# First two batches' last queries beside their last keys, w_ch1 behind the values, and the first four batches' pieces and loads in another order

## The chip, the cores and the metric

The kernel runs on one core of a Trainium2 chip. A core has TensorE for matmuls (PE in the profile; PEld is its weight load), VectorE (DVE), ScalarE (ACT), GpSimd (POOL) and SyncE (SP, which here only issues DMAs), 16 DMA engines, an on-chip memory SBUF of 128 partitions and an accumulator memory PSUM that matmuls write to. Each engine works through its own list of instructions in order and waits on semaphores. The metric is the device time of one execution in microseconds (us); lower is better.

## The reference

Linear attention with a cosine weighting, then a mixer over tokens and channels, for 8 batches of 576 tokens, 8 heads of 64.

```python
def phi(x, c, s):                       # c, s: cosine and sine of the token's place
    r = np.maximum(x, 0.0)
    return np.concatenate([r * c, r * s], axis=-1)
q_p = phi(q, cos_w, sin_w)
k_p = phi(k, cos_w, sin_w)
kv = np.einsum('bhsf,bhsd->bhfd', k_p, v)
z = np.sum(k_p, axis=2)
num = np.einsum('bhsf,bhfd->bhsd', q_p, kv)
den = np.einsum('bhsf,bhf->bhs', q_p, z)[..., None] + 1e-06
x = num / den                           # then 576 tokens x 512 channels for each batch
xt = x.transpose(0, 2, 1)
h = np.maximum(xt @ w_tok1, 0.0) @ w_tok2      # 576 -> 256 -> 576
u = x + h.transpose(0, 2, 1)
h2 = np.maximum(u @ w_ch1, 0.0) @ w_ch2        # 512 -> 1536 -> 512
out = u + h2
```

Inputs and outputs are float32; matmuls are bfloat16 with float32 sums.

## The kernel before, in words

**Tiles.** The 576 tokens of a batch are four chunks (0 to 3) of 128 and a tail (R) of 64. The tails of two batches share one tile of 128 partitions: rows 0 to 63 for the even batch, 64 to 127 for the odd one (`half(b % 2)`). `kp`, `qp` are the features of keys and queries (128 for a head), `v_aug` the values with a column of ones, so that `kv_ps` carries the sum of keys too. `qpT` are the turned queries, `x` the attention output, `B` the inner tokens of the mixer, `u` the residual, `uT` its transpose, `h1T` the inner channels (12 of them, `NCH`).

**Stages.** Batch b's channel mixer (`Channel`) is a list of steps: 12 of `c_step` (four matmuls of 512 columns into `c_ps`, then ScalarE's `h1T`; odd batches also carry the tail pair's `c_tail`), then `o_step` pieces of two matmuls. Batch b+1's attention and token mixer (`Front.pieces`) is cut into pieces, and a plan says at which slot (step) of batch b each is issued; C is slot 0 and O slot 12. So the order on every engine is written out by hand. KS and QS make the features of a chunk of keys or queries (cosine and sine half; with True the sine half goes to ScalarE), V casts values, KV adds a chunk to `kv_ps`, QT turns queries on TensorE, `q_trans_dma` by a DMA issued from SP, N makes `num_ps` and x, `mix_head` and `mix_tail` are the first token product, T the second with `u`, and `u_trans_dma` makes `uT`. Even and odd batches have plans of their own; batch 2, whose loads come late, has the plan "late" with V at slots 6, 6, 7, 7, 7 and KV at 7, 7, 8, 8, 8, where the odd plan has V at -1, -1, 0, 1, 2 and KV at 2 to 6.

**The first front.** Batch 0's attention has no stage to lie beside; `first_front` writes it out: q features and TensorE transposes in halves of four heads, the q tail, the keys chunk by chunk with `ksum`, then `dens` (q times the key sum, all 40 columns into `d_ps`), kv by halves of the heads (lo on ScalarE, hi on VectorE to `kv_sb`), five `num` with the x multiplication on VectorE, tok1, B, transposes to `uT` and the first three `c_ps` by blocks. `busy` issues matmuls of zeros that fill TensorE's pauses.

**Loads.** SP's queue issues most loads; w_ch1 and w_ch2, which are cast on the way, go through GpSimd's queue. `after` makes one load wait for another: w_ch1 for the second half of k 0, batch 1's k for the second part of w_ch1, batch 2's k for the second of three parts of w_ch2. `load_batch` is called at given steps. PSUM has four banks in `ps_mm` and two pairs in `ps_at`.

Of the kernel before, what the change touches and what calls it, by code (L numbers as in the profile page):

```python
# [16 lines left out]
def kernel(  # L17
# [76 lines left out]

    def tiles():
        return tuple(io.tile([P, H, R * D], F32, name=n) for n in ("qt", "vt", "kt"))
# [9 lines left out]
    load_tail(qtt0, q, 0)  # L106
    load_main(kt0, k, 0, 0, HH)
    k_done = load_main(kt0, k, 0, HH, H)
# [3 lines left out]
    load_main(vt0, v, 0, HH, H)  # L112
# [3 lines left out]
    w_tok1n = stage1[:, 0:R * D_tok].rearrange("p (r t) -> p r t", r=R)  # L116
    w_tok2n = stage2[:, 0:NT * S].rearrange("p (n s) -> p n s", n=NT)
# [37 lines left out]
    v_augs, x_tails = [], []  # L155
    for i in range(2):
        va = const.tile([P, NSC, H, DP], BF16, name=f"v_aug{i}")
        nc.vector.memset(va[:, 0:R, :, D:D1], 1.0)
        nc.vector.memset(va[half(1 - i), R, :, :], 0.0)
        nc.vector.memset(va[half(i), R, :, D:D1], 1.0)  # L160
        v_augs.append(va)
        xt = const.tile([P, Dm], BF16, name=f"x_tail{i}")
        nc.vector.memset(xt[half(1 - i), :], 0.0)
        x_tails.append(xt)
# [15 lines left out]
    for t in (tail0.kp, tail0.qp):  # L180
        nc.gpsimd.memset(t[half(1)], 0.0)
    for g in range(2):
        nc.gpsimd.dma_start(out=w_tail1[half(g), :], in_=moe_w_tok1[SM:S, :])
# [8 lines left out]
    after(w_ch1_done[0], k_done)  # L192
    w_ch2_done = []
    def load_w_ch2(third):
        ki = third * NCH // 3
        w_ch2_done.append(nc.gpsimd.dma_start(
            out=w_ch2[:, ki:ki + 4, :],
            in_=moe_w_ch2[ki * P:(ki + 4) * P, :].rearrange("(n t) d -> t n d", t=P)))
# [10 lines left out]
    def permute_tok2(ki):  # L209
        nc.scalar.copy(w_tok2[:, ki, 0:SM].rearrange("t (r p) -> t r p", r=R),  # L210
                       w_tok2n[:, ki, 0:SM].rearrange("t (p r) -> t r p", r=R))
        nc.scalar.copy(w_tok2[:, ki, SM:].rearrange("t (g s) -> t g s", g=2),
                       w_tok2n[:, ki, None, SM:S].to_broadcast([P, 2, ST]))


    class Front:
        def __init__(self, b, res, tail):
            self.qt, self.vt, self.kt = io_tiles[b]
            self.va, self.xt = v_augs[b % 2], x_tails[b % 2]
            self.res, self.tail = res, tail  # L220
            self.rows = half(b % 2)


            self.alone = b < 2
            self.kp, self.qp = {}, {}
# [20 lines left out]
        def feature(self, which, ci, j, heads=(0, H), on_act=False):  # L246
# [8 lines left out]
            else:  # L255
                t = self.tail
                dst, src = (t.kp, t.kt) if which == "k" else (t.qp, t.qt)
                rows = self.rows if self.alone else slice(0, P)
                w, o_ap, i_ap = w[rows], dst[rows, lo:hi, j, :], src[rows, lo:hi, :]
            if on_act:  # L260
                nc.scalar.activation(o_ap, i_ap, AF.Relu, bias=bias0[0:w.shape[0]], scale=w)
# [33 lines left out]
        def dens(self, ci):  # L295

            if ci == 0:
                self.d_ps = ps_mm.tile([P, NSC * H], F32, name="d_ps", tag="mm")
                self.d_sb = small.tile([P, NSC * H, 1], F32, name="d_sb")
            for h in range(H):  # L300
                i = ci * H + h
                nc.tensor.matmul(self.d_ps[:, i:i + 1], self.qT_of(ci, h),
                                 self.ks_sb[:, h:h + 1], start=True, stop=True)

        def dens_out(self, lo, hi):
            nc.vector.tensor_scalar_add(self.d_sb[:, lo:hi, 0], self.d_ps[:, lo:hi], 1e-6)
            nc.vector.reciprocal(self.d_sb[:, lo:hi, 0], self.d_sb[:, lo:hi, 0])

        def kv(self, ci, halves=(0, 1)):
            if ci == 0 and not hasattr(self, "kv_ps"):  # L310
                self.kv_ps = {}
                if halves == (0, 1):
                    both = ps_at.tile([P, 2, 512], F32, name="kv_ps", tag="at")
                    self.kv_ps = {g: both[:, g, :] for g in range(2)}
            if ci == 0 and halves != (0, 1):
                for g in halves:
                    self.kv_ps[g] = ps_at.tile([P, 2, 512], F32, name="kv_ps", tag="at")[:, 0, :]
# [10 lines left out]
        def kv_out(self, halves=(0, 1)):  # L328
            for g in halves:
                copy = nc.vector.tensor_copy if g else nc.scalar.copy  # L330
# [16 lines left out]

        def q_trans_dma(self, ci):
# [4 lines left out]
        def num(self, ci, fill=0, dens=False):  # L353
            num_ps = ps_at.tile([P, 2, 512], F32, name="num_ps", tag="at")
            if fill:
                busy(num_ps[:, 0, HH * DP:512], 1)
            for h in range(H):
                g, j = divmod(h, HH)
                nc.tensor.matmul(num_ps[:, g, j * DP:j * DP + D1], self.qT_of(ci, h),  # L359
                                 self.kv_sb[g][:, j, 0:D1], start=True, stop=True)  # L360
            rows = self.rows_of(ci)
            nv = num_ps[rows, :, 0:HH * DP].rearrange("p g (j d) -> p g j d", d=DP)
            if dens:
                den = self.d_sb[rows, ci * H:(ci + 1) * H, :].rearrange("p (g j) o -> p g j o", g=2)
            else:
# [3 lines left out]
            nc.vector.tensor_mul(  # L369
                self.x_of(ci)[rows].rearrange("p (g j d) -> p g j d", g=2, j=HH),  # L370
                nv[:, :, :, 0:D], den.to_broadcast([rows.stop - rows.start, 2, HH, D]))
# [89 lines left out]
        def pieces(self, b, before):  # L461
# [3 lines left out]
            first, odd, late = b == 1, b % 2 == 1, b == 2  # L465
# [3 lines left out]
            if first:  # L469

                u, act, pool = before.tok2, nc.scalar, nc.gpsimd
                plan = [(4, KS, 0), (4, KS, 1), (5, u, 0, ps_at, False), (5, KS, 2, True),
                        (6, KS, 3, True), (6, u, 1, ps_at, False), (7, KS, R), (7, V, R, nc.vector), (8, V, 0, act),
                        (8, V, 2, pool), (8, load_w_ch2, 0), (8, V, 3, pool),
                        (8, load_w_ch2, 1), (8, load_w_ch2, 2),
                        (8, u, 2, None, False), (9, V, 1, act), (9, u, 3, None, False),
                        (9, QS, 0), (10, u, R, None, False)]
                plan += [(11, KV, ci) for ci in range(NSC)]
                plan += [(11, QS, 1), (11, QS, 2), (11, self.kv_out),
                         (11, QT, 0, (0, H), act, ps_at), (11, QT, 1), (11, QS, R),  # L480
                         (O, QT, 2), (O, N, 0), (O, QS, 3), (O + 1, QT, R),
                         (O + 1, N, 1), (O + 3, N, 2), (O + 3, QT, 3),
                         (O + 5, N, R), (O + 7, N, 3), (O + 8, before.tail_cast)]
            else:
# [21 lines left out]
            if first:  # L506
                at, mix, t = (), O + 7, O + 11
            elif odd:
                at, mix, t = (C + 8, C + 9, C + 10, C + 11, O + 2), O + 3, O + 7
            elif late:  # L510
                at, mix, t = (C + 10, C + 11, O + 1, O + 2, O + 4), O + 5, O + 9
# [20 lines left out]
    class Channel:  # L532
# [59 lines left out]
        def steps(self, done):  # L592
# [43 lines left out]
    def first_front(f):  # L636
# [24 lines left out]
        busy(idle_ps, 2)  # L661
        f.ksum(R)
        busy(idle_ps, 1)
        for ci in range(R):
            if ci == 2:
                f.ksum_out()
            f.values(ci, nc.scalar, lo_heads)
        cast_tok1(0)
        f.values(R, nc.vector)
        for ci in range(R):  # L670
            f.values(ci, nc.vector, hi_heads)
        for ci in (0, 1, 2):
            f.dens(ci)
# [3 lines left out]
        for ci in (R, 3):  # L677
            f.dens(ci)
        f.dens_out(0, NSC * H)
# [9 lines left out]
        f.num(ORDER[0], fill=1, dens=True)  # L689
        f.num(ORDER[1], dens=True)  # L690
# [23 lines left out]
    def load_batch(b, which="kvq", behind=None, main=True, tails=True):  # L714
# [7 lines left out]
        for n in which:  # L722
# [7 lines left out]
            if tails and (b % 2 == 0 or b == 1):  # L730
                load_tail(tail_dst, src, b | 1)
        return done
# [3 lines left out]
    load_batch(1, "kvq", behind=w_ch1_done[1])  # L736
# [9 lines left out]
    c = first_front(fronts[0])  # L746
    slots = next_front(1)
    for b in range(B):
# [4 lines left out]
        for i, step in enumerate(steps):  # L753
# [54 lines left out]
```

## Time and profile before

| | us |
|---|---|
| median of 3 runs (269.6 to 270.21) | 270.06 |
| profiled execution, its own time | 270.61 |
| its span, first to last instruction | 268.8 |
| TensorE busy | 260.0 (97%) |
| VectorE busy | 164.9 (61%) |
| ScalarE busy | 129.9 (48%) |
| GpSimd busy | 10.9 (4%) |
| TensorE on the chain that ended last | 86% |
| DMA, mean over the span | 200 GB/s |
| granted TensorE clock | 1.00 |

A page of the profile comes from one execution. Busy time is the union of an engine's instructions; a matmul's end is modelled, so back-to-back matmuls overlap by some 0.2 us in the records, and the pace is read from start to start. The chain is followed back from the last instruction to what released it. In the timeline each row has start, duration, engine, line of the kernel, instruction, out<-in, shape and count; what stands in brackets is the engine's idle time before it and what ended it. A DMA's time to landing counts from its issue.

### The profile page before, as it was taken

The page shows a single profiled execution, that of the slowest core. Times are in us where ns is not written, and L with a number is a line of the kernel's source. Part 1 is how long each engine was busy: PE and PEld are TensorE (multiplying, and loading weights), DVE is VectorE, ACT ScalarE, POOL GpSimd, SP SyncE. Part 2 cuts the span into 40 slices and gives each one's busy share as a digit, 9 for nine tenths or more (in the row PEclk, how much of TensorE's full clock was granted, in tenths as well). Part 3 has the DMA queues.
Part 4 walks back from the last instruction along what each step waited for, and adds up shares of the span by engine and source line. Part 5 has one row for each costly group of instructions (what it writes and reads, how often), then busy time and mean ns, then how long its engine had stood idle before and what let it go on. Part 6 is the DMA issues. An engine that isn't in the chain of part 4 may idle for free.

```text
span 268.8 us, 5101 instructions
## 1 busy us (share of the span) xinstructions
PE 260.0 (97%) x2029; PEld 139.2 (52%) x2050; DVE 164.9 (61%) x376; ACT 129.9 (48%) x228; POOL 10.9 (4%) x24
## 2 busy tenths in 40 slices
PE   7989999999999999999999999999999999999994
PEld 2565465455544455446644455446644455445543
DVE  6874798794366747777466747776565846720022
ACT  4954975528606272446606372546606362526400
POOL 6300220000000000000000000000000000000000
PEclk9999999999999999999999999999999999999999
DMA  6999999589999999469984989189974580180032
GB/s 217 342 277 275 333 162 285 211 210 253 179 316 289 251 208 319 146 166 266 182 307 117 287 207 355 54 179 254 229 261 117 156 120 0 53 202 3 2 107 88
DMA packets 91815, 53.68 MB, mean 200 GB/s; under 512 B 59408, under 2 KB 86928, under 8 KB 91792
## 3 DMA queue, kind: packets, MB, share of 16 engines
q1 hardware_dynamic: 88432, 49.62, 69.5%
q0 software_dynamic: 2832, 3.21, 7.2%
q10 hardware_dynamic: 528, 0.52, 0.6%
q8 instruction: 16, 0.26, 0.4%
q14 instruction: 7, 0.06, 0.1%
HBM read 35.85 MB, written 9.44 MB: 168 GB/s over the span
## 4 chain that ended last, share of the span: by engine, by line
PE 86%; DVE 6%; DMA 3%; ACT 3%; issue 1%; DVEq 0%; ACTq 0%
PE o_ps L579 33%; PE c_ps L546 25%; PE u_ps L406 7%; PE b_ps L382 6%; PE ct_ps L566 3%; PE kv_ps L320 3%; PE num_ps L359 3%; DVE x_sb L369 3%; DMA qt<-in_q_dram 2%; DVE qp L263 1%; ACT h1T L550 1%; PE qT_ps L340 1%; DMA qpT_tail<-qp_tail 1%; PE idle_ps L204 1%; ACT v_aug L274 1%; PE c_ps L556 1%
## 5 line engine op out<-in xcount | busy, mean ns | idle before, releaser
L579 PE MATMUL o_ps<-w_ch,h1T 128*128 128x512 bf16 (+1 forms) x380 | 92.6, 372 | 0.6
L546 PE MATMUL c_ps<-uT,w_ch 128*128 128x512 bf16 (+2 forms) x384 | 92.2, 372 | 0.1
L550 ACT ACTIVATE h1T<-c_ps 128x512 bf16<-128x512 f32 x93 | 55.5, 599 | 60.5 <-PE c_ps L546 60.1
L579 PEld LDWEIGHTS <-h1T 128*128 128x128 bf16 x396 | 37.3, 98 | 39.5 <-issue 0.2
L546 PEld LDWEIGHTS <-w_ch 128*128 128x128 bf16 x384 | 33.5, 97 | 29.5 <-issue 0.2
L584 DVE TENSOR_TENSOR o_sb<-o_ps,u_sb 128x512 f32<-128x512 f32 (+1 forms) x33 | 22.3, 674 | 29.5 <-PE o_ps L579 29.4
L409 DVE TENSOR_TENSOR u_sb<-u_ps,x_sb 128x512 f32<-128x512 f32 x32 | 21.7, 689 | 6.0 <-PE u_ps L406 5.6
L413 ACT CAST u_bf<-u_sb 128x512 bf16<-128x512 f32 x28 | 17.3, 620 | 16.7 <-DVE u_sb L409 16.7
L406 PE MATMUL u_ps<-B,w_tok 128*128 128x512 bf16 x79 | 22.4, 379 | 0.2
L387 ACT ACTIVATE B<-b_ps 128x512 bf16<-128x512 f32 x8 | 4.8, 598 | 33.7 <-PE b_ps L382 33.5
L369 DVE TENSOR_TENSOR x_sb<-num_ps,den 128x512 bf16<-128x512 f32 x28 | 19.4, 691 | 1.0
L566 PEld LDWEIGHTS <-w_ch 128*128 128x128 bf16 x192 | 14.0, 98 | 9.2
L382 PE MATMUL b_ps<-x_sb,w_tok 128*128 128x512 bf16 x63 | 17.7, 379 | 0.1
L263 DVE TENSOR_SCALAR kp<-kt,cos_t 128x512 bf16<-128x512 f32 x32 | 15.2, 481 | 3.8 <-DMA kt<-in_k_dram 3.8
L566 PE MATMUL ct_ps<-uT_tail,w_ch 128*128 128x128 bf16 x192 | 17.2, 219 | 0.0
L274 ACT CAST v_aug<-vt 128x512 bf16<-128x512 f32 (+1 forms) x30 | 16.8, 587 | 0.1
L263 DVE TENSOR_SCALAR qp<-qt,cos_t 128x512 bf16<-128x512 f32 (+1 forms) x35 | 15.9, 455 | 0.5 <-DMA qt<-in_q_dram 0.5
L263 DVE TENSOR_SCALAR qp<-qt,sin_t 128x512 bf16<-128x512 f32 (+1 forms) x35 | 15.9, 455 | 0.0
L359 PEld LDWEIGHTS <-qpT 128*128 128x128 bf16 x256 | 11.5, 98 | 6.1 <-issue 1.1
L584 DVE TENSOR_TENSOR o_sb<-o_ps,u_tail 128x512 f32<-128x512 f32 x4 | 2.8, 692 | 19.0 <-PE o_ps L579 19.0
L359 PE MATMUL num_ps<-kv_sb,qpT 128*128 128x65 bf16 x256 | 13.0, 193 | 1.3 <-DVE x_sb L369 0.5
L331 DVE CAST kv_sb<-kv_ps 128x260 bf16<-128x260 f32 x8 | 3.5, 433 | 16.6 <-ACT kv_sb L331 16.5
(93 smaller groups left out, 228.6 us busy)
## 6 DMA issues: line engine op xcount, KB each, us to landing
out_dram<-o_sb SPq DMA_DIRECT2D x31, 256.0 KB, 2.9
kt<-in_k_dram SPq DMA_DIRECT2D x7, 1024.0 KB, 6.6
vt<-in_v_dram SPq DMA_DIRECT2D x7, 1024.0 KB, 6.6
qt<-in_q_dram SPq DMA_DIRECT2D x7, 1024.0 KB, 8.4
w_ch<-in_moe_w_ch_dram POOLq DMA_DIRECT2D x4, 384.0 KB, 10.2
w_ch<-in_moe_w_ch_dram POOLq DMA_DIRECT2D x3, 512.0 KB, 7.5
out_dram<-o_sb SPq DMA_DIRECT2D x10, 128.0 KB, 2.3
qtt<-in_q_dram SPq DMA_DIRECT2D x8, 128.0 KB, 5.3
```

The source lines that it names most:

```text
L263: nc.vector.tensor_scalar(o_ap, i_ap, scalar1=w, scalar2=0.0, op0=ALU.mult, op1=ALU.max)
L274: nc.scalar.copy(dst, src)
L359: nc.tensor.matmul(num_ps[:, g, j * DP:j * DP + D1], self.qT_of(ci, h), self.kv_sb[g][:, j, 0:D1], start=True, stop=True)
L369: nc.vector.tensor_mul(self.x_of(ci)[rows].rearrange("p (g j d) -> p g j d", g=2, j=HH), nv[:, :, :, 0:D], den.to_broadcast([rows.stop - r ...
L382: nc.tensor.matmul(self.b1_ps[mi], w, self.x_of(ci), start=(ci == ORDER[0]), stop=(ci == ORDER[-1]))
L406: nc.tensor.matmul(u_ps, w_tok2[:, ki, ci * P:(ci + 1) * P], self.B1[:, ki, :], start=(ki == 0), stop=(ki == NT - 1))
L409: nc.vector.tensor_add(u, u_ps[rows], self.x_of(ci)[rows])
L546: nc.tensor.matmul(c_ps[:, lo:hi], w_ch1[:, ki, mi * P:(mi + 1) * P], uT[:, lo // P:hi // P, ki, :], start=(ki == 0), stop=(ki == NCC - 1))
L550: nc.scalar.activation(self.h1T[:, mi, :], c_ps, AF.Relu)
L566: nc.tensor.matmul(self.ct_ps[:, mi % R, :], w_ch1[:, ki, mi * P:(mi + 1) * P], self.tail.uT[:, ki, :], start=(mi % R == 0 and ki == 0), s ...
L579: nc.tensor.matmul(o_ps, h, w_ch2[:, ki, cols], start=ki == 0, stop=ki == NCH - 1)
L584: nc.vector.tensor_add(o_sb, o_ps, u)
```

## The change

Batch 0's and 1's query tails no longer have a tile and a pass of their own: `load_beside` puts them into the free half of the key tail's tile, the key features of the tail run on all 128 rows, and `q_trans_beside` turns the other half's rows with transposes of 64 columns. In the first front the keys follow the queries at once, chunk 0 in halves; the sines of chunks 1 to 3 are ScalarE's; the value casts, `kv_sb` copies and weight casts are shared among VectorE, ScalarE and GpSimd in another way; `dens` runs in one piece before kv, and the first two chunks' `num` and x are made by halves of the heads. w_tok1's tail is loaded by SP in float32 and cast by GpSimd; w_ch1 waits for the values instead of the keys. In batch 0's stage the five tok2 pieces come first, keys and values a slot or more later, q 0's sine goes to ScalarE, w_ch2 comes in four parts, and the first two o chunks alternate by one step instead of two. Batch 3 gets the late plan; the late plan's QS R moves from slot 6 to 9. The loads of batches 2, 3 and 4 change places: batch 2's q tail behind the first turned queries, batch 3's v from step 9 to step 24 of batch 1, batch 4's k from there to step 4 of batch 2.

The diff, cut to its core:

```diff
+    def load_beside(dst, src, b):
+        return nc.sync.dma_start(out=dst[half(1 - b)],
+                                 in_=src[b, :, SM:S, :].rearrange("h s d -> s h d"))
...
-    load_tail(qtt0, q, 0)
+    load_beside(ktt0, q, 0)
...
+    for g in range(2):
+        nc.sync.dma_start(out=w_tail1n[half(g), :], in_=moe_w_tok1[SM:S, :])
...
-    after(w_ch1_done[0], k_done)
+    after(w_ch1_done[0], v_done)
...
+        def q_trans_beside(self):
+
+            g = self.rows.start // ST
+            rows = half(1 - g)
+            qT_ps = ps_mm.tile([P, H, ST], BF16, name="qT_ps", tag="mm")
+            for h in range(H):
+                nc.tensor.transpose(qT_ps[:, h, :],
+                                    self.tail.kp[rows, h, :, :].rearrange("p a b -> p (a b)"),
+                                    ident[rows, rows])
+            nc.scalar.copy(self.tail.qpT[:, :, half(g)], qT_ps)
...
-            first, odd, late = b == 1, b % 2 == 1, b == 2
+            first, odd, late = b == 1, b % 2 == 1, b in (2, 3)
...
-                plan = [(4, KS, 0), (4, KS, 1), (5, u, 0, ps_at, False), (5, KS, 2, True),
-                        (6, KS, 3, True), (6, u, 1, ps_at, False), (7, KS, R), (7, V, R, nc.vector), (8, V, 0, act),
-                        (8, V, 2, pool), (8, load_w_ch2, 0), (8, V, 3, pool),
-                        (8, load_w_ch2, 1), (8, load_w_ch2, 2),
-                        (8, u, 2, None, False), (9, V, 1, act), (9, u, 3, None, False),
-                        (9, QS, 0), (10, u, R, None, False)]
+                plan = [(4, u, 0, ps_at, False), (5, u, 1, ps_at, False), (5, KS, 0),
+                        (6, u, 2, None, False), (6, KS, 1), (7, u, 3, None, False),
+                        (7, KS, 2, True), (8, u, R, None, False), (8, KS, 3, True),
+                        (9, V, R, nc.vector), (9, KS, R), (9, V, 0, act),
+                        (10, V, 2, pool), (10, load_w_ch2, 0, 2), (10, V, 3, pool),
+                        (10, load_w_ch2, 2, 4), (10, load_w_ch2, 4, 8),
+                        (10, load_w_ch2, 8, NCH), (10, V, 1, act), (11, QS, 0, True)]
...
-                             (2, QS, 1), (3, QS, 2), (4, QS, 3), (5, KS, R), (6, QS, R))
+                             (2, QS, 1), (3, QS, 2), (4, QS, 3), (5, KS, R), (9, QS, R))
...
-                for lo in range(0, NCH, 4):
+                for lo in range(0, NCH, 2):
                     for ci in (0, 1):
-                        o_range(ci, lo, lo + 4)
+                        o_range(ci, lo, lo + 2)
...
-        f.q_side(R)
-        f.q_trans(R, pool=ps_at)
-        busy(idle_ps, 2)
-        for ci in range(R):
+        for heads in (lo_heads, hi_heads):
+            f.feature("k", 0, 0, heads)
+            f.feature("k", 0, 1, heads)
+        busy(idle_ps, 4)
+        f.ksum(0)
+        for ci in range(1, R):
             f.feature("k", ci, 0)
-            f.feature("k", ci, 1, on_act=(ci > 1))
-            busy(idle_ps, 2)
+            f.feature("k", ci, 1, on_act=True)
+            busy(idle_ps, 2 if ci < 3 else 1)
             f.ksum(ci)
         f.k_side(R)
...
+        f.ksum_out()
+        f.q_trans_beside()
         for ci in range(R):
...
+            f.values(ci, nc.vector if ci < 2 else nc.scalar, lo_heads)
         f.values(R, nc.vector)
         for ci in range(R):
-            f.values(ci, nc.vector, hi_heads)
...
+            f.values(ci, nc.vector if ci < 3 else nc.scalar, hi_heads)
+        den = f.dens(range(NSC))
+        f.dens_out(*den)
         for ci in range(NSC):
             f.kv(ci, (0,))
         f.kv_out((0,))
...
-        f.kv_out((1,))
-        cast_tok1(1)
-        for ki in range(NT):
-            permute_tok2(ki)
+        f.kv_out((1,), on_act=(1,))
+        for ci in ORDER[:2]:
+            f.num(ci, dens=True, halves=(0,), pool=ps_mm, fill=1)
+        for ci in ORDER[:2]:
+            f.num(ci, dens=True, halves=(1,), fill=1)
+        for mi in range(NT):
+            cast_tok1(mi)
+        permute_tok2(0, nc.scalar.copy)
+        nc.gpsimd.tensor_copy(w_tail1, w_tail1n)
+        permute_tok2(1, nc.gpsimd.tensor_copy)
+        fill_fixed(1, nc.gpsimd)
...
+            if b == 1 and n == "k":
+                load_beside(ktt, q, b)
...
-                load_batch(2, "kq", behind=w_ch2_done[1], tails=False)
+                load_batch(2, "kq", behind=w_ch2_done[2], tails=False)
             if b == 0 and i == NCH + 13:
-                load_batch(2, "v", tails=False)
-                load_batch(2, "kqv", main=False)
+                load_batch(2, "v")
+                load_batch(2, "k", main=False)
+            if b == 1 and i == 1:
+                load_batch(2, "q", main=False)
             if b == 1 and i == 9:
-                load_batch(3, "kvq")
+                load_batch(3, "kq")
+            if b == 1 and i == NCH + 12:
+                load_batch(3, "v")
+            if b == 2 and i == NSC - 1:
+                load_batch(4, "k")
             if 1 < b < B - 2 and i == NSC:
                 load_batch(b + 2, "vq")
-            if 0 < b < B - 3 and i == NCH + 12:
+            if 1 < b < B - 3 and i == NCH + 12:
                 load_batch(b + 3, "k")
```

More of the change, by code (lines that the diff above doesn't have):

```diff
@@ L179 @@
     tail0 = Tail(0)
[L180 to L183, printed above, removed]
+    nc.gpsimd.memset(tail0.qpT[:, :, half(1)], 0.0)
     C2 = D_ch // 2
@@ L351, in q_trans_dma, with num @@
                                         in_=self.q_of(ci).rearrange("p h a b -> p (h a b)"))
[L353 to L362, printed above, removed]
+        def num(self, ci, dens=False, halves=(0, 1), pool=ps_at, fill=0):
+            shape, tag = ([P, 2, 512], "at") if pool is ps_at else ([P, 1, 512], "mm")
+            num_ps = pool.tile(shape, F32, name="num_ps", tag=tag)
+            busy(num_ps[:, 0, HH * DP:512], fill)
+            for g in halves:
+                for j in range(HH):
+                    nc.tensor.matmul(num_ps[:, g - halves[0], j * DP:j * DP + D1],
+                                     self.qT_of(ci, g * HH + j),
+                                     self.kv_sb[g][:, j, 0:D1], start=True, stop=True)
+            rows, n = self.rows_of(ci), len(halves)
+            nv = num_ps[rows, 0:n, 0:HH * DP].rearrange("p g (j d) -> p g j d", d=DP)
             if dens:
-                den = self.d_sb[rows, ci * H:(ci + 1) * H, :].rearrange("p (g j) o -> p g j o", g=2)
+                den = self.d_sb[ci][rows].rearrange("p (g j) o -> p g j o", g=2)
+                den = den[:, halves[0]:halves[-1] + 1]
             else:
@@ L368, in num @@
                 nc.vector.reciprocal(den, den)
[L369 to L371 removed]
+            x = self.x_of(ci)[rows].rearrange("p (g j d) -> p g j d", g=2, j=HH)
+            nc.vector.tensor_mul(x[:, halves[0]:halves[-1] + 1], nv[:, :, :, 0:D],
+                                 den.to_broadcast([rows.stop - rows.start, n, HH, D]))
         def tok1(self, mi, chunks):
@@ L746 @@
     c = first_front(fronts[0])
+    load_batch(1, "kvq", behind=w_ch1_done[1])
     slots = next_front(1)
```

113 lines of the change are left out of this document (48 added, 65 removed).

## The prediction

> **What bounds the kernel now.** I read the table of stages first, cut where a batch's first channel product (`c_ps`) starts; its columns are the stretch in us, its length, busy time and count of each engine, granted clock, DMA share and GB/s.
>
> ```profile
> core 0: us, PE busy (x) PEld busy (x) DVE busy (x) ACT busy (x) POOL busy (x), PEclk, DMA share, GB/s
> 0.00:24.45 24.45, 21.11 (x266) 12.83 (x269) 17.46 (x52) 16.23 (x31) 7.36 (x19) 1.00 1.00 269
> 24.45:56.34 31.89, 31.68 (x243) 17.00 (x246) 25.43 (x55) 18.93 (x30) 3.55 (x5) 1.00 0.96 252
> 56.34:91.04 34.70, 33.60 (x267) 18.44 (x269) 20.86 (x47) 16.11 (x29) 0.00 (x0) 1.00 1.00 250
> 91.04:118.54 27.50, 27.39 (x195) 13.78 (x196) 18.86 (x42) 13.71 (x24) 0.00 (x0) 1.00 0.95 223
> ...
> 178.80:211.50 32.70, 32.59 (x255) 17.63 (x256) 20.93 (x47) 14.96 (x27) 0.00 (x0) 1.00 0.81 208
> ```
>
> From 24.45 on TensorE (PE) sets the pace at the full clock: a change pays only where PE waits. Batch 1's stage has the work of batch 5's (32.70) and takes 2.00 longer, so that much at most is to be had there; batch 2's takes 27.50, like batch 4's and 6's, so there is nothing to win and something to lose. DMA is full until about 49. The first 24.45 is a chain over all engines, read from the timeline (start, duration, instruction):
>
> ```profile
> 14.90 0.74 PE L302 MATMUL d_ps<-ks_sb,qpT 128*128 128x1 bf16 x24
> ...
> 17.32 0.43 DVE L331 CAST kv_sb<-kv_ps 128x260 bf16<-128x260 f32 x1
> ...
> 18.12 1.89 DVE L369 TENSOR_TENSOR x_sb<-num_ps,d_sb 128x512 bf16<-128x512 f32 x3 [0.37 <-PE num_ps L359]
> ...
> 20.66 0.69 DVE L369 TENSOR_TENSOR x_sb<-num_ps,d_sb 128x512 bf16<-128x512 f32 x1
> ```
>
> The five x multiplications end at 21.35 and start only after the second `kv_sb`. Last, the timeline of ScalarE (ACT) in the stages of batches 0 and 1, then of PE in the latter:
>
> ```profile
> 31.62 0.80 ACT L261 ACTIVATE kp<-kt,bias,sin_t 128x512 bf16<-128x512 f32 x1
> 32.42 0.60 ACT L550 ACTIVATE h1T<-c_ps 128x512 bf16<-128x512 f32 x1
> 33.28 0.60 ACT L550 ACTIVATE h1T<-c_ps 128x512 bf16<-128x512 f32 x1 [0.27 <-PE c_ps L546]
> ```
>
> ```profile
> 63.75 0.60 ACT L550 ACTIVATE h1T<-c_ps 128x512 bf16<-128x512 f32 x1
> 64.37 1.14 ACT L274 CAST v_aug<-vt 128x512 bf16<-128x512 f32 x2
> 65.41 0.59 ACT L550 ACTIVATE h1T<-c_ps 128x512 bf16<-128x512 f32 x1
> 65.90 1.13 ACT L274 CAST v_aug<-vt 128x512 bf16<-128x512 f32 x2
> 66.93 0.62 ACT L274 CAST v_aug<-vtt 64x512 bf16<-64x512 f32 x1
> ```
>
> ```profile
> 65.04 0.92 PE L320 MATMUL kv_ps<-v_aug,kp 128*128 128x65 bf16 x16
> ...
> 66.89 0.65 PE L320 MATMUL kv_ps<-v_aug,kp 128*128 128x65 bf16 x16
> ```
>
> Start to start an `h1T` costs ACT 0.50, a sine 0.80, a value cast 0.55 to 0.6. In batch 1's stage, where the "late" plan bunches five casts in slots 6 and 7, every kv group starts right behind its cast: PE loses about 0.7 there.
>
> Sums are made against the profiled execution: 270.61, of which 268.8 is the span; the median of the runs, 270.06, lies 0.55 below, and I add the same difference to it. The measurement can tell about 0.2%, 0.54 us, from no change.
>
> **First front.** The two tail-query features on VectorE (DVE; 0.8 together), eight transposes and ACT's 1.01 copy at 10.76 leave the path between q and k. DVE ends q at 9.1; k's chunk 0 goes in halves (0.26 each, as the q halves) by the landings, 8.65 and 10.57, to 11.1; cosines of chunks 1 to 3 (0.39) to 12.3; the tail pair on 128 rows to 13.15 (64 rows took 0.47, 128 take 0.49: the q rows ride free). ACT's three sines (0.76 each) run from 10.66 to 12.98. So `ks_ps` ends near 13.5, `ks_sb` 13.7, and dens starts at 13.8, not 14.90; the 64-column transposes fill PE's wait for `ks_sb`. Forty dens (0.027 each) end at 14.9, kv's lo half at 15.5, hi at 16.0 (20 times 0.028; ACT's last value cast ends about 15.5). ACT copies lo by 15.95 and hi by 16.46, where DVE's hi copy ended at 17.75. Num's lo halves start meanwhile: four half multiplications from 16.4. None is in the trace; they cost between 0.30 (half of the full spacing 0.60) and 0.45, and I take 0.33, near the casts, where halving goes from 0.39 to 0.22. They end at 17.7; the three full ones, at 0.65 with their bank waits, at 19.87. Gain 1.48 (bounds 1.0 and 1.8); the 3.05 from the last tok1 to the first `c_ps` stays, so that one starts at 22.97.
>
> Covers: the tok1 casts end at 17.7, before x 0 is through; GpSimd's (POOL's) casts (0.60 to 0.79 for 128x512) run from 17.4 and are needed at 19.4 and 21.2. w_ch1's four issues (0.80 each) wait for the values' landing, 14.20 instead of 10.57. At the old delays (8.6 and 9.7) the first two land at 22.8 and 24.7, and PE would wait 0.4; at the old pace of 1.88 between landings behind the shorter queue they land near 18 and 20. I take no wait, as DMA is full either way, and keep 0.4 for the range. Batch 1's k load still follows the second.
>
> **Batch 0's channel stage.** Slots 4 to 8 carry the tok2 pieces (0.43 of PE beside c's 0.86), slots 7 and 8 each an ACT sine, slots 9 and 10 a value cast, slot 11 a new sine for q 0. Counting ACT from `h1T` 7 at 31.36: five `h1T` 2.5, three sines 2.4, two casts 1.2, so q 0's sine ends at 37.5. PE reaches kv 1 at 35.70 and waits for its cast until 36.2, then would reach the transposes of q 0 at 36.6 without waits and starts them at 37.53: +0.90 (before, PE never waited there; bounds 0.3 and 1.1). Behind that sine on ACT stand `kv_sb` and the `qpT` copies, which num 0 needs. The tail transposes at 64 columns cost 0.03 instead of 0.053, minus 0.2, with 0.1 lost on a PSUM bank: net -0.10. w_ch2's later parts are needed near 41.9 and 45.0 and landed at 41.63 and 44.90, bound by the full DMA: +0.10 (0 to 0.4).
>
> **Batch 1's stage.** PE waited 0.61 for the first transposed queries (landed 70.57) and 0.38 for the tail's (74.52). The two qtt loads now stand behind the first transpose on SP, so that one is issued about 1.9 earlier and its wait ends; next late is the tail's transpose, behind the same transfers as before. Gain between 0 (it lands as before) and 0.99; I take 0.40. The q tail features move to slot 9, behind `kv_sb` on DVE; nothing is queued there before num's den.
> By the Trainium skill, DMA: Bandwidth & Descriptors (Queues, rings and completion order), each DMA engine consumes a ring's descriptors in order. The five landings about 1 us apart in issue order agree; by that alone this gain is 0 and the sum 0.4 worse.
>
> **Batch 2's stage.** Batch 3 now has the late plan, so its five casts leave slots -1 to 2 for 6 and 7, and here a slot has no 0.22 of tail products. From the stage's start, c 6 ends at 6.05 and c 7 at 6.91; ACT: `h1T` 6 at 6.25 (0.2 behind), casts ready 7.37 and 7.9, `h1T` 7 at 7.86, casts ready 8.9, 9.4, 10.0. PE: kv 0 at 7.43, kv 1 7.97 to 8.19, c 8 to 9.05, kv 2 to 9.27, kv 3 9.54, the tail 10.06 to 10.28; unhindered it is 8.87. Cost +1.41 (0.7, as in batch 1, to 1.8). Batch 4's k moves into this stage (1.2 MB), and tok2 moves two steps towards its end: `uT` landed 1.4 before its need; +0.10 (0 to 0.6). Value loads of batch 3 follow `uT`, land near 94, needed at 97.
>
> Sum: -1.48 + 0.90 - 0.10 + 0.10 - 0.40 + 1.41 + 0.10 = **+0.53**: 271.14 in a profiled run, **270.6** at the median.
>
> **Rivals.** (a) *ScalarE's backlog is smaller than counted.* It is priced twice, 0.90 and 1.41; from a quarter less than that on (0.53) the change no longer loses, at half the time is 270.06 + 0.53 - 1.15 = 269.4, with none 268.3. For it: ACT idles 0.19 to 0.27 ahead of most `h1T` in batch 0's stage; against it: the kv rows above. (b) *Transfers come late*: w_ch2's last parts, batch 1's tail transpose and batch 3's `uT` all stand behind full queues; at their far bounds (0.3 + 0.4 + 0.5) 271.8, already 271.2 at half. (c) *GpSimd holds VectorE.* DVE's 64x512 value cast took 0.83 beside a POOL cast and 0.45 alone; if POOL's new copies held the x chain alike, twice 0.38 gives 271.4. No row shows an x multiplication beside POOL.
> The Trainium skill, SBUF — State Buffer (the shared port pair), says a GpSimd instruction shuts out DVE only in a two-port mode or with two SBUF inputs; x reads PSUM and one SBUF tile, so by it the chain is free, which keeps this chance small.
> (d) *The front gains nothing*, something else ending it at 21.35: 272.1. (e) The parts cancel and nothing shows: 270.1.
>
> **Chances.** The sum as made, 0.40 (own range 270.1 to 271.1, about evenly across the 0.54 bound); (a) 0.28; (b) 0.16; (c) 0.06; (d) 0.06; (e) 0.04. Faster: (a) and a little of the sum's edge, 0.32; within 0.2%: half of the sum, (e) and a bit of (b), 0.24; slower 0.44. The range 268.9 to 271.9 leaves out (a) at its full price and (d), some 2 in 10 with the edges.
>
> **What would show it.** Right: the first `c_ps` at about 23.0, q 0's transposes late behind ACT's sine, batch 1's stage near 34.3, batch 2's near 28.9 with PE waiting on `v_aug`, later stages as now. Wrong: batch 2's stage still 27.5 (then (a)); waits on `w_ch` or `uT` (then (b)); x ending near 21 (then (c) or (d)).

## The result, and the profile after

The changed kernel takes 272.94 us (median of 4 runs, 272.31 to 275.39), the kernel before 270.08 on the same chip (269.60 to 270.21). The ratio is 1.0128, with a 95% interval of 1.0096 to 1.0160: 2.9 us slower, outside the forecast range of 268.9 to 271.9. The changed kernel also scatters more. Its profiled execution is the slowest of the four (275.39, span 273.6). A second profile, from the runs below, has 272.62 and a span of 270.83. Ratios are of fast runs alone; all runs here and below are fast but one of `w2_earlier` (275.76).

The table of stages of the profile after is cut where each batch's first `c_ps` starts:

```profile
0.00:24.16 24.16, 21.79 (x267) 13.27 (x268) 15.19 (x49) 15.08 (x30) 7.72 (x23) 1.00 0.98 259
24.16:60.76 36.60, 32.97 (x247) 17.00 (x246) 24.21 (x52) 18.98 (x31) 4.53 (x6) 1.00 0.93 231
60.76:94.61 33.85, 33.57 (x269) 18.43 (x268) 20.64 (x47) 15.06 (x27) 0.00 (x0) 1.00 0.89 224
94.61:123.41 28.80, 28.11 (x197) 13.95 (x196) 18.57 (x42) 14.81 (x26) 0.00 (x0) 1.00 0.98 254
```

Against the kernel before, the first front gains 0.29, batch 0's stage loses 4.71, batch 1's gains 0.85 and batch 2's loses 1.30; all later stages agree within 0.1. So the loss is in batch 0's stage, where 0.90 had been forecast. TensorE is busy 32.97 of 36.60 there; before, it was 31.68 of 31.89. The timeline of that stage shows who waits for what (the last bracket is the idle time ahead of the instruction, and what ended it):

```profile
35.66 0.61 POOL L279 CAST v_aug<-vt 128x512 bf16<-128x512 f32 x1 [14.85 <-DMA vt<-in_v_dram]
...
36.21 0.72 POOL L202 DMA_DIRECT2D w_ch<-in_moe_w_ch_dram  x1
...
37.76 2.43 POOL L202 DMA_DIRECT2D w_ch<-in_moe_w_ch_dram  x3
...
38.46 0.82 ACT L264 ACTIVATE qp<-qt,bias,sin_t 128x512 bf16<-128x512 f32 x1 [0.70 <-DMA qt<-in_q_dram]
...
44.20 1.02 PE L595 MATMUL o_ps<-w_ch,h1T 128*128 128x512 bf16 x4 [1.36 <-DMA w_ch<-in_moe_w_ch_dram]
...
47.19 1.02 PE L595 MATMUL o_ps<-w_ch,h1T 128*128 128x512 bf16 x4 [1.28 <-DMA w_ch<-in_moe_w_ch_dram]
```

Batch 1's values land at 35.53 (before: 31.92). GpSimd casts one chunk of them and only then asks for `w_ch2`, at 36.21 (before: 32.61). TensorE waits twice for that weight, 1.52 and 1.44 from matmul to matmul. Before, it did not wait there. The page's chain that ended last says the same in one line; DMA stood at 3% before:

```profile
PE 78%; DMA 12%; ACT 3%; SPq 3%; POOL 1%; issue 0%; POOLq 0%; DVE 0%; ACTq 0%
```

The first front in the profile after, to be held against the chain shown in the prediction:

```profile
14.15 0.95 PE L304 MATMUL d_ps<-ks_sb,qpT 128*128 128x1 bf16 x32
...
16.80 1.42 DVE L385 TENSOR_TENSOR x_sb<-num_ps,d_sb 128x256 bf16<-128x256 f32 x4 [0.80 <-PE num_ps L372]
...
18.38 0.69 DVE L385 TENSOR_TENSOR x_sb<-num_ps,d_sb 128x512 bf16<-128x512 f32 x1 [0.16 <-PE num_ps L372]
...
19.30 0.35 PE L372 MATMUL num_ps<-kv_sb,qpT_tail 128*128 128x65 bf16 x6 [0.47 <-issue]
...
19.70 0.68 DVE L385 TENSOR_TENSOR x_tail<-num_ps,d_sb 64x512 bf16<-64x512 f32 x1 [0.62 <-PE num_ps L372]
```

The four half multiplications start 0.33 to 0.34 apart (16.80, 17.14, 17.47 and 17.80 in the trace), as was taken (0.33). The first full one starts 0.58 behind the last of them, having waited 0.16 for its product. The tail's product is held up 0.6 by an "issue" gap on TensorE, in the middle of eight matmuls that wait for nothing shown.

Batch 2's stage, where batch 3's value casts now stand in slots 6 and 7:

```profile
101.35 1.13 ACT L277 CAST v_aug<-vt 128x512 bf16<-128x512 f32 x2
102.01 0.92 PE L322 MATMUL kv_ps<-v_aug,kp 128*128 128x65 bf16 x16 [0.33 <-ACT v_aug L277]
...
102.86 1.13 ACT L277 CAST v_aug<-vt 128x512 bf16<-128x512 f32 x2
103.63 0.82 PE L322 MATMUL kv_ps<-v_aug,kp 128*128 128x65 bf16 x16
104.02 0.61 ACT L277 CAST v_aug<-vtt 64x512 bf16<-64x512 f32 x1
...
104.69 0.40 PE L322 MATMUL kv_ps<-v_aug,kp_tail 128*128 128x65 bf16 x8 [0.24 <-ACT v_aug L277]
```

Each kv group starts behind its cast, as in batch 1's stage before. That is the forecast picture.

### The profile page after: what moved, and what is told of

It reads as the page before. It is cut to its first block, busy times and chain, and to the rows that moved or that the text cites. A ratio compares the mean times of both kernels' runs of the same rounds, so it can differ in the third digit from the quotient of the medians.

```text
span 273.6 us, 5126 instructions
## 1 busy us (share of the span) xinstructions
PE 263.1 (96%) x2049; PEld 139.7 (51%) x2049; DVE 160.9 (59%) x370; ACT 128.8 (47%) x228; POOL 12.3 (4%) x29
## 4 chain that ended last, share of the span: by engine, by line
PE 78%; DMA 12%; ACT 3%; SPq 3%; POOL 1%; issue 0%; POOLq 0%; DVE 0%; ACTq 0%
PE o_ps L595 34%; PE c_ps L562 25%; DMA vt<-in_v_dram 6%; DMA w_ch<-in_moe_w_ch_dram 6%; PE u_ps L421 6%; PE b_ps L397 6%; PE ct_ps L582 4%; PE num_ps L372 3%; PE kv_ps L322 2%; ACT v_aug L277 2%; SPq L86 1%; ACT h1T L566 1%; SPq L92 1%; SPq L98 1%; POOL v_aug L279 1%
## 5 line engine op out<-in xcount | busy, mean ns | idle before, releaser
L595 PE MATMUL o_ps<-w_ch,h1T 128*128 128x512 bf16 (+1 forms) x396 | 94.4, 372 | 2.6 <-DMA w_ch<-in_moe_w_ch_dram 2.6
L595 PEld LDWEIGHTS <-h1T 128*128 128x128 bf16 x396 | 37.2, 97 | 41.9 <-issue 2.9
L277 ACT CAST v_aug<-vt 128x512 bf16<-128x512 f32 (+1 forms) x29 | 16.2, 594 | 0.1
L266 DVE TENSOR_SCALAR kp<-kt,cos_t 128x512 bf16<-128x512 f32 (+1 forms) x33 | 15.4, 472 | 0.6 <-DMA kt<-in_k_dram 0.6
```

The lines of the kernel that those rows point to most:

```text
L277: nc.scalar.copy(dst, src)
L595: nc.tensor.matmul(o_ps, h, w_ch2[:, ki, cols], start=ki == 0, stop=ki == NCH - 1)
```

## The experiments

All are edits of the changed kernel unless said otherwise. Time is the median, and the ratio is that against the kernel before on the same chip. In every profile I read when the first eight of `w_ch2`'s twelve chunks had landed, and when batch 0's stage ended; the table stands behind `front_later`.

**again**: no edit.

> The changed kernel once more, on the same chip as the three that follow. Theory T (transfers): the stage of batch 0 loses its time to loads, w_ch1 being asked for 3.7 us later, so batch 1's k, v and q land 2.1 to 3.6 us later and w_ch2, which GpSimd asks for behind its cast of these values, 1.8 to 2.5 later; the profile should show PE waiting for w_ch2 again (1.52 and 1.44 us before), though by how much may vary, and the time stays at 272 to 275. Theory A (ScalarE's backlog, as predicted): batch 0's stage is long through ACT's own queue, about 0.9 us, and the w_ch2 waits were an accident of one execution and are below 0.5 now.

Measured: 273.62 us (272.62 to 274.15), ratio 1.0130 [1.0109, 1.0152]. TensorE waits 0.31 and 1.27 for `w_ch2`; batch 0's stage is 34.36. The weight is late in another execution too, so ScalarE's backlog is not the main cause. A table of single microseconds of this profile shows a stretch in which little is moved, while `w_ch1` has just been asked for:

```profile
15.00:16.00 1.00, 1.00 (x39) 1.00 (x37) 0.60 (x2) 0.76 (x4) 1.00 (x3) 1.00 1.20 392
16.00:17.00 1.00, 1.00 (x30) 0.87 (x27) 0.32 (x1) 0.78 (x3) 1.00 (x2) 1.00 1.00 122
17.00:18.00 1.00, 0.57 (x16) 0.48 (x15) 1.00 (x4) 1.00 (x3) 0.89 (x3) 1.00 1.05 184
```

The last column falls from 392 to 122 GB/s for a microsecond; the kernel before moved 268 there. The DMA share beside it is still 1.00, so by the profile the DMA engines were not idle in it.

**w1_behind_k**:

```diff
-    after(w_ch1_done[0], v_done)
+    after(w_ch1_done[0], k_done)
```

> The changed kernel, but w_ch1 waits for the keys' second half again (10.3 us), as before the change, not for the values (14.2). Theory T: batch 1's loads and w_ch2 land as before the change (k 28.4, v 31.9, q 35.1, last w_ch2 near 45 to 46), the waits for w_ch2 and for q are gone, batch 0's stage is 32 to 33 us and the time 270.0 to 270.8. Theory A: the stage keeps some 0.9 us of waits behind ACT's sine although q has landed 2 us earlier, and the time stays near 272.5. If what was gained in the first front hangs on w_ch1's being late, its end goes from 24.2 back to 24.5 or later.

Measured: 272.57 us, ratio 1.0091 [1.0067, 1.0114]. The stretch of 122 GB/s is gone, but batch 1's values land at 33.68, no earlier than in `again` (33.16), and TensorE waits 1.58 for `w_ch2`. Theory T as I wrote it falls: in this profile the late request for `w_ch1` does not by itself delay the rest. The median is 1.05 below `again`'s, with intervals that just overlap, and the profile is the slowest of the six runs, so a smaller part is not ruled out.

**k1_earlier**:

```diff
-    load_batch(1, "kvq", behind=w_ch1_done[1])
+    load_batch(1, "kvq", behind=w_ch1_done[0])
```

> The changed kernel, but batch 1's first load waits for the first part of w_ch1, not for the second: it is asked for about 2.0 us earlier (20.2, not 22.1), with w_ch1 still behind the values. Theory T: the delay is handed on through batch 1's loads, so values land near 34, w_ch2 is asked for 1.5 us earlier, and 1.0 to 2.0 us of the loss goes: 271.0 to 272.0; at most 0.3 comes back as a wait for the last parts of w_ch1. A rival within T: the transfer rate alone decides (the same bytes between 15 and 50 us), then w_ch1 lands that much later, w_ch2 as late as now, and the time stays at 272.9. Theory A: no change, 272.9.

Measured: 272.52 us, ratio 1.0091 [1.0071, 1.0111]. The keys are asked for at 19.41 but land at 29.56, and the values at 33.07; the wait for `w_ch2` is 1.11. Also less than theory T asked for: 271.0 to 272.0.

**w1_k1_early**: both of these edits together.

> The changed kernel with both of the earlier edits: w_ch1 behind the keys and batch 1's first load behind the first part of w_ch1, so that no hole is left in the transfers between 15 and 30. Theory T3 (the hole of 1 to 2 us and the later request for the keys delay batch 1's values, each hiding the other's gain in w1_behind_k and k1_earlier): the values land at 32.0 to 32.5, w_ch2 8 of 12 chunks at 43.0, the wait for it falls below 0.8 and the time to 271.8. The rival (what stands ahead of the values is the same amount at the same rate, and 0.4 to 0.6 of it is the tail queries' load): values at 33 to 33.7 as in both, time 272.5.

Measured: 272.06 us, ratio 1.0078 [1.0048, 1.0108]. The values land at 32.08, eight chunks of `w_ch2` at 42.92, under 0.1 of wait for it is left, and batch 0's stage is 32.85. Landings and wait are as theory T3 had them, the time is 0.3 above its number. That fits T3, in which each edit alone hides behind the other's delay. The interval still overlaps those of the single edits, so T3 rests on the profile and not on the medians. What remains in the stage is ScalarE's backlog: 0.39 for `v_aug`, 0.24 for the query's sine, 0.18 for a `qpT` copy.

**w2_earlier**: GpSimd asks for `w_ch2` ahead of its casts.

```diff
+        if len(w_ch2_done) == 1:
+            after(w_ch2_done[0], first_loads[1])    # batch 1's tail queries
...
-  (10, V, 2, pool), (10, load_w_ch2, 0, 2), (10, V, 3, pool), (10, load_w_ch2, 2, 4), ...
+  (10, load_w_ch2, 0, 2), (10, load_w_ch2, 2, 4), (10, load_w_ch2, 4, 8),
+  (10, load_w_ch2, 8, NCH), (10, V, 2, pool), (10, V, 3, pool), ...
```

> The changed kernel, but GpSimd asks for w_ch2 ahead of its two value casts, as soon as batch 1's tail queries have landed (near 30.3), and not behind the first cast, which waits for batch 1's values (34.1). Theory T2: the hole in the transfers behind batch 1's queries (share 0.1 to 0.4 for a microsecond, at 35) is filled, w_ch2 lands 1 to 2 us earlier, the waits for it fall from 1.3 to 2.9 us to below 0.5, and the time is 271.3 to 272.0. The rival (the transfers are full either way): values and queries of batch 1 land later by what w_ch2 lands earlier, TensorE waits for these instead, and the time stays near 273.

Measured: 272.37 us (271.0 to 272.67, and one run at 275.76), ratio 1.0080 [1.0055, 1.0105], which does not meet `again`'s interval. Eight chunks land at 41.37, the wait for them is gone, and the stage is 32.69:

```profile
24.32:57.01 32.69, 32.38 (x247) 16.93 (x246) 23.67 (x52) 18.98 (x31) 4.23 (x6) 1.00 0.96 254
```

That is 0.80 above the 31.89 of before, in an execution in which TensorE waited neither for `w_ch2` nor for the queries' landing: ScalarE's price, undisturbed. Its waits are 0.39 for `v_aug`, 0.24 for the query's sine and 0.18 for a `qpT` copy. The queries pay for the earlier weight: they land at 37.75, not 36.12. The median is 0.4 above the range that was expected; this profile's front was long (24.32) for another reason, told at the end.

**w2_earlier_dve**: also `(8, KS, 3)` and `(11, QS, 0)` without `True`, so that these sines are VectorE's.

> As w2_earlier, and the sines of batch 1's key chunk 3 and query chunk 0 are on VectorE, not on ScalarE. Theory A's part (the backlog on ScalarE, waits of 0.39 for v_aug, 0.24 for the query sine and 0.12 for qpT, forecast at 0.90): with w_ch2 out of the way these 0.75 us are gone too, 0.5 to 0.8 less than w_earlier's time. Theory T2 alone (transfers set the end whatever the engines do): within 0.2 us of w2_earlier. If VectorE is late instead, the waits are for qp or kv_sb from VectorE and nothing is won.

Measured: 273.49 us, ratio 1.0140 [1.0100, 1.0180]. Nothing is won. TensorE now waits 0.61 and 0.34 for `qp` from VectorE, which has both products of that query chunk to make once the queries have landed, at 37.94; the 0.39 for `v_aug` stays.

**front_later**: the front's gain taken away again.

```diff
+        late = ps_mm.tile([P, SM], F32, name="late", tag="mm")
+        busy(late, 4)
         for kb in range(NCC):
```

> The changed kernel with four more dummy matmuls of 512 columns (0.21 each) on TensorE between the last tok1 and the turning of x in the first front: its first c_ps starts 0.85 us later, and nothing else is touched. Theory T2 (w_ch2's landing sets the end of batch 0's stage, since it hangs on loads and not on TensorE): batch 0's stage gets shorter by what the front is longer, the time stays that of the changed kernel (272.9 to 273.6), and the time won in the front is worth nothing. The rival (TensorE's own order of work is the bound and the waits for w_ch2 only add to it): 0.85 more, about 274.3.

Measured: 273.70 us, ratio 1.0144 [1.0115, 1.0173]; `again` had 1.0130. The two intervals leave the difference anywhere from about -0.6 to +1.4 us, so the time alone does not decide it. Here are all profiles (us from the span's start; `batch1_only`, below, has the first front and batch 0's stage of the kernel before):

| profile | first `c_ps` | eight chunks landed | wait for them | stage ends | end less landing |
|---|---|---|---|---|---|
| before | 24.45 | 41.63 | 0 | 56.34 | 14.71 |
| before_again | 24.27 | 43.33 | 0.67 | 56.83 | 13.50 |
| batch1_only | 24.44 | 42.51 | 0 | 56.34 | 13.83 |
| after | 24.16 | 47.15 | 1.44 | 60.76 | 13.61 |
| again | 23.57 | 44.22 | 1.27 | 57.93 | 13.71 |
| w1_behind_k | 24.11 | 44.86 | 1.58 | 58.47 | 13.61 |
| k1_earlier | 23.37 | 43.56 | 1.11 | 57.17 | 13.61 |
| batch3_as_before | 23.13 | 44.59 | 1.41 | 58.20 | 13.61 |
| front_later | 23.98 | 45.32 | 1.54 | 59.00 | 13.68 |
| w1_k1_early | 23.77 | 42.92 | 0.08 | 56.62 | 13.70 |
| w2_earlier | 24.32 | 41.37 | 0 | 57.01 | 15.64 |
| w2_earlier_dve | 24.17 | 43.04 | 0 | 57.39 | 14.35 |
| both_batch3 | 23.57 | 41.28 | 0 | 56.83 | 15.55 |
| best_try | 24.32 | 42.22 | 0 | 57.16 | 14.94 |

Wherever TensorE waits for the eighth chunk, the stage ends 13.5 to 13.7 behind its landing, whether the first `c_ps` starts at 23.13 or at 24.27. The landing sets the end there, and what the front gained is spent in the wait. front_later fits the row: its front is 0.85 longer than batch3_as_before's, and its stage still ends 13.68 behind the landing. But the landing itself is 0.73 later than there, and the stage (35.02) is not shorter than `again`'s, as theory T2 had it. That the landing stays where it is when the front moves is not shown by one profile in which it moved.

**batch3_as_before**: batch 3's plan and loads as they were.

```diff
-            first, odd, late = b == 1, b % 2 == 1, b in (2, 3)
+            first, odd, late = b == 1, b % 2 == 1, b == 2
...
-                load_batch(3, "kq")          # and "v", batch 4's "k" in later steps
+                load_batch(3, "kvq")         # and batch 4's "k" at NCH + 12, as before
```

> The changed kernel, but batch 3 has the plan and the loads that it had before (its value casts in slots -1 to 2 of batch 2's stage, k, v and q asked for together in batch 1's, batch 4's k at the end of batch 1's). If the late plan of batch 3 is what makes batch 2's stage 28.80 instead of 27.50, it is 27.5 again and the time 1.3 us less: 271.6. The rival: the 1.3 is a cost of tok2's two later steps or of batch 4's k, or batch 1's stage pays instead (33.85 goes to 34.7, as before): then the time is within 0.5 of the changed kernel's.

Measured: 271.91 us, ratio 1.0067 [1.0043, 1.0092], 0.6% below `again`; 0.5% (1.3 us) was expected. The stage of batch 2 is 27.50 without a wait, and batch 1's 34.27:

```profile
92.47:119.97 27.50, 27.50 (x198) 13.78 (x197) 18.84 (x42) 13.69 (x24) 0.00 (x0) 1.00 0.95 229
```

So 1.30 of the loss is batch 3's late plan with its loads, which the edit takes back together. Nothing comes back for it that can be told from the scatter: batch 1's stage is 33.7 to 34.5 in the eight profiles with the late plan and 34.1 to 34.6 in the three without.

**both_batch3**: w2_earlier_dve and batch3_as_before together.

> As w2_earlier_dve, and batch 3 with the plan and loads that it had before (batch 2's stage 27.5). If the three costs are separate (w_ch2's wait, ScalarE's backlog, batch 3's late plan), they add up: front 23.1 to 23.6, batch 0's stage 32.0 to 32.6, batch 1's 34.3, batch 2's 27.5, and the time is 268.8 to 269.8, below the kernel before (270.1). If transfers push one into the other, above 270.5.

Measured: 270.68 us, ratio 1.0047 [1.0023, 1.0071]; batch 0's stage is 33.26, with the waits for VectorE's `qp` (0.66 and 0.34) in it. The weight's wait and batch 3's price are gone as expected. The sum (268.8 to 269.8) failed with the VectorE edit and with the queries, which land at 37.38, 1.26 later than in `again`; above 270.5 is where the rival, transfers that push one into the other, had put the time.

**best_try**: w1_k1_early and batch3_as_before, and the first four chunks of `w_ch2` ahead of GpSimd's casts.

```diff
-  (10, V, 2, pool), (10, load_w_ch2, 0, 2), (10, V, 3, pool), (10, load_w_ch2, 2, 4), (10, load_w_ch2, 4, 8),
+  (10, load_w_ch2, 0, 2), (10, load_w_ch2, 2, 4), (10, V, 2, pool), (10, V, 3, pool), (10, load_w_ch2, 4, 8),
```

> The changed kernel with w_ch1 behind the keys, batch 1's loads behind the first part of w_ch1, the first four chunks of w_ch2 asked for ahead of GpSimd's casts (behind the tail queries), the other eight behind them, and batch 3 as before. If the costs add up: front 23.3, batch 0's stage 32.7 (ScalarE's waits of 0.8 stay), batch 1's 34.3, batch 2's 27.5, 0.6 to 1.0 below the kernel before: 269.0 to 269.5. If batch 1's queries are pushed back again (37.4 to 37.9 in the runs that asked for w_ch2 early), 0.5 to 1.0 more, level with the kernel before.

Measured: 270.72 us, ratio 1.0022 [1.0001, 1.0043]: level with the kernel before or just above it. That is the second case of what was expected: the queries were pushed back to 37.93. The front took 24.32. No version here beats the kernel before.

**batch1_only**: the kernel before, with this one part of the change.

```diff
-                load_batch(2, "v", tails=False)
-                load_batch(2, "kqv", main=False)
+                load_batch(2, "v")
+                load_batch(2, "k", main=False)
+            if b == 1 and i == 1:
+                load_batch(2, "q", main=False)
...
-  (5, KS, R), (6, QS, R)
+  (5, KS, R), (9, QS, R)
```

> The kernel before with one part of the change alone: the tail loads of batches 2 and 3 in the new order (values' with the values, keys' next, the queries' two behind the first transposed queries on SP's queue) and the tail query features in slot 9. By the prediction's step for batch 1's stage (0.40, up to 0.99): the first transposed queries land 1.5 us or more earlier, their wait of 0.61 is gone, and the stage goes from 34.7 to between 34.1 and 34.4 (the tail's transpose, behind the same transfers, is waited for by 0.4 to 0.8), everything else as before; the time is 0.3 to 0.6 below the kernel before's, 269.4. The rival (landings in order, gain 0): 34.7 and the kernel before's time.

Measured: 269.86 us against 269.83, ratio 0.9994 [0.9975, 1.0012]. In the profile batch 1's stage is 33.68 and both waits for transposed queries are gone, and yet the median has not moved. Neither expectation held, so the kernel before was profiled once more.

**before_again**: the kernel before.

> The kernel before, profiled a second time. In batch1_only the waits of batch 1's stage were gone (33.69, not 34.69) and yet the median stayed. If the profiled execution of before was an unlucky one, in which the first transposed queries landed late, this profile has a stage of 33.7 to 34.3 and a span of 267.8 to 268.4; if the waits are there in every execution of the kernel before, it has 34.7 and 268.8 again, and batch1_only lost its gain somewhere else.

Measured: 270.09 us, span 268.3. Its table of stages:

```profile
24.27:56.83 32.56, 31.84 (x243) 17.01 (x246) 25.50 (x55) 18.92 (x30) 3.55 (x5) 1.00 0.97 247
56.83:90.52 33.69, 33.26 (x267) 18.50 (x269) 20.74 (x47) 16.09 (x29) 0.00 (x0) 1.00 0.97 259
```

Batch 1's stage is 33.69 here without any edit. The first transposed queries landed at 68.39 (70.57 in the first profile). The two waits that the prediction meant to remove belong to one execution. This profile waits 0.67 for `w_ch2` instead, so in this execution of the kernel before that landing has no slack to give either.

## Why the prediction was wrong

**The step that failed: `w_ch2`, +0.10 (0 to 0.4).** Measured: 1.1 to 3.0 us of waits in six of the seven profiles of the changed kernel and its edits in which the request stayed behind GpSimd's cast (the seventh is w1_k1_early). The step left the landings where they were before, "bound by the full DMA", and they moved: the eighth chunk lands at 42.92 to 47.15 in these seven profiles, and at 41.63, 42.51 and 43.33 in the three with the old loads. The part on `w_ch1` had asked only whether TensorE would wait for `w_ch1` itself (it never does), and not what the new order does to the loads behind it.

The times of need in the step do not stand in the profile of before either. The matmul that waits for the eighth chunk starts there at 42.88, not at 41.9, and its request is the first of the two in the first row:

```profile
34.12 1.49 POOL L196 DMA_DIRECT2D w_ch<-in_moe_w_ch_dram  x2
...
42.88 1.03 PE L579 MATMUL o_ps<-w_ch,h1T 128*128 128x512 bf16 x3
```

The next part is first used at 45.95, not at 45.0. Both are 1.0 earlier in the step, more than the 0.7 by which the sum moves TensorE (1.48 - 0.90 + 0.10). So the slack before was 1.25 in this profile, where the step had 0.3; it was 0.36 in batch1_only and none in before_again, which waits 0.67. A landing that moves by 1.7 among three executions of the same loads could not be taken from one of them.

Two parts of the delay can be read. GpSimd asks for `w_ch2` behind a cast that waits for batch 1's values, and these land at 32.08 to 35.53, not at 31.84 to 32.33. And the request for the part with the eighth chunk goes out 2.8 to 3.2 behind the values' landing, not 2.2: `w_ch2` comes in four parts, so it is the third request and no longer the second. From this request to the landing it takes 7.5 to 8.7, and 7.5 to 9.3 with the old loads. No run takes the four parts back, so what these 0.6 to 1.0 are worth is open.

What puts the values off is not settled. w1_k1_early, which has no slow stretch at 16 to 17 and asks for the keys at 19.12, lands the values 1.1 and the weight 1.3 earlier than `again`. But `again` asks for the keys at 21.46, hardly later than the kernel before (21.39 and 21.32), so an earlier request makes up for the delay and does not name its cause. The load of the tail queries, which now stands between keys and values, adds 0.35 to 0.66 between their landings. Why the first profile lost 3.6 us there stays open too.

So it was the second rival, "transfers come late", that happened. It named what was waited for, but its far bound gave `w_ch2` 0.3 more where 1 to 3 were lost.

**The front, -1.48 (1.0 to 1.8).** Over the ten profiles with the changed front as it is, the first `c_ps` starts at 23.13 to 24.32, at 23.85 in the mean; in three with the old front it starts at 24.27 to 24.45, at 24.39 in the mean. That is a gain of 0.5, a third of what was forecast. In the four that nothing held up (23.13, 23.37 and two of 23.57) the gain is 0.7 to 1.3. The others were held up by the issue gap (0.56 to 0.71), by the tail weights' cast (0.54) or by the clock. The half multiplications cost what was taken; the step's own figures (17.7 and three at 0.65) give 19.7 and not 19.87. None of this decided: wherever TensorE then waits for `w_ch2`, the stage ends by the landing whatever the front gained.

**ScalarE's backlog, +0.90 less 0.10.** Measured by itself in w2_earlier: +0.80, which is the sum of the three waits named there. In the first profile the same sine waited for the queries' landing, so it could not be read there.

**Batch 1's stage, -0.40 (0 to 0.99).** 33.7 to 34.6 in the profiles with the new order, 34.69 and 33.69 in two profiles of before: no gain that can be measured. The step took two waits of a single execution, out of a profile 0.55 above the median, for waits of the kernel.
The bound of 0, for which the Trainium skill, DMA: Bandwidth & Descriptors (Queues, rings and completion order) was cited, came true in the time, but not by that rule. The landings of batch1_only do come in the order of issue, which agrees with it; the first transpose, moved ahead of two loads, lands at 66.51, and both waits are gone.

**Batch 2's stage, +1.41 (0.7 to 1.8).** +1.30 to +1.35 in each of eight profiles with the late plan, gone in the three without it. The count by slots was right (+1.41); the 0.10 for `uT` did not appear.

Put together, against before_again (268.3): the second profile of the change has -0.70 for the front, +1.80 for batch 0's stage, +0.19 for batch 1's, +1.30 for batch 2's, -0.07 later; span +2.5. The medians lie 2.9 to 3.5 apart. The rest is in executions that were not profiled, and stays open. The ten runs of the changed kernel spread over 3 us (272.31 to 275.39); the kernel before spread over 1.0, 1.8 and 2.4 us in three comparisons of 16, 17 and 24 runs (269.34 to 271.76 in all).

## What to carry to other kernels

Before a gain is put into a sum, look along the path for the next landing that does not move with it, and read from the trace when the matmul that waits for it starts: the gain is worth no more than the slack there. Here that slack was 1.25 us in one profile of the old loads, 0.36 in another and none in a third. When a load is put off, follow every load that is released by it, through the casts and requests that stand behind them on other engines, down to the last weight. And take a wait out of a profile for a property of the kernel only if a second profile, or the distance of the profile from the median, bears it out.

## What the runs showed of the hardware

In three of eleven profiles with the changed front the granted clock of TensorE fell to one half for 3.41 us, from 14.46, 14.66 and 15.09 on; in best_try:

```profile
14.00:18.00 4.00, 4.00 (x92) 3.97 (x89) 1.75 (x7) 2.54 (x8) 0.18 (x1) 0.57 1.12 283
```

There, sixteen kv matmuls took 1.04 instead of the 0.65 of `again`, and the three fronts took 24.2 to 24.3. It is no rare event: of the 83 executions with the changed front, 42 have a mean granted clock of 0.988 to 0.994 (0.994 in these three profiles), and none of 71 with the old front has less than 0.997.

The clock records of the traces hold a step. In the three profiles the full clock is first granted at 4.22, 4.42 and 4.84, and it falls 10.24 later in each, three times 3.41. In the other eight it is first granted at 5.76 to 7.21 and stays. So where these steps lie goes with the fall; what sets it off is open, as two profiles of the kernel before were granted the clock at 4.24 and 4.41 and kept it. By the Trainium skill, TensorE: Matmul & The Clock Gate (What's actually happening), the gate looks at activity in a free-running window, which would make it differ from run to run as here; the steps of 3.41 agree with such a window.
